# A key-value product with its high and low parts side by side, and a softmax-free attention's denominators in other places

## The chip, the cores and the metric

The kernel runs on one core of a Trainium2 chip. A core has a matrix engine (TensorE, PE in the profile, with its weight loads shown apart as PEld), a vector engine (VectorE, DVE), an activation engine (ScalarE, ACT), a general engine (GpSimd, POOL), and a sync engine (SyncE, SP) that issues the transfers here. Each engine works through its own queue in order; semaphores make one queue wait for another. The metric is device time in microseconds (us) of one execution, as the median of several runs.

## What is computed

One transformer block with adaptive layer norm, on a sequence of 2048 tokens with 512 channels, in fp32. Its first half is linear attention with 32 heads of 16 channels:

```python
pq, pk = phi(q), phi(k)                 # phi(t) = (t + 1 if t > 0 else exp(t)) + 1e-6
kv  = einsum("bhsd,bhse->bhde", pk, v)  # one 16 x 16 matrix per head
z   = einsum("bhsd->bhd", pk)
num = einsum("bhqd,bhde->bhqe", pq, kv)
den = einsum("bhqd,bhd->bhq", pq, z) + 1e-6
x   = x + ga * ((num / den) @ wo)
```

The second half is a gated feed-forward layer, `x + gb * (((h @ w_gate) * (h @ w_up)) @ w_down)`, with h the normalised and modulated x again. The vectors sa, ca, ga, sb, cb, gb come from `silu(c) @ w_mod`.

## The kernel before

**Precision.** A matrix product of fp32 values is made of three products in a rounded 32-bit format (fp32r). Each operand is split into a high part, which ScalarE writes by a copy into fp32r, and a low part, which VectorE writes as the difference (`split`, lines 193 to 195). `product` (lines 203 to 209) then adds, for each block of the contraction, high by high (line 207), high by low (208) and low by high (209) in one PSUM bank.

**Tiles.** The sequence is 16 tiles of 128 tokens, in four chunks of four. Work on tile i of the queries is called q tile i here. Tiles in SBUF come from one pool of 94 buffers of 128 x 512 fp32; PSUM is four accumulator banks (`acc`) and four working banks (`bank`). A working bank is handed out again when its last reader is done, so a new product can wait for a VectorE instruction that reads an old one.

**Order.** Nothing is scheduled by a planner in this part: the program is written in the order in which each engine gets its instructions, and an engine's queue is the sequence of its instructions in the text. A step late on one queue holds all that stands behind it there.

**The stretch that matters** begins after the last key tile. The key side has by then accumulated, in four banks `tacc[k]`, the normalised input against phi(k), which with the value weights gives kv without ever forming v. The steps, with their lines:

- `den_z` (671 to 673) reduces the key sums zb to a constant part of the denominators.
- Lines 779 and 780 scale `tacc[k]` into four tiles f; line 784 splits each of these into a high and a low part, `tt[k]`, each 128 x 512.
- The key-value product, lines 788 to 791: for each group g of 128 output columns, and each block k, the three products of 128 columns each. That is 4 x 4 x 3 = 48 matrix products of 128 x 128 by 128 x 128, into the one bank `kvps`.
- `mod_row` (line 792, by 183 and 189) makes the row gb: two products of 512 columns and one ScalarE copy.
- `q_b` (line 376) ends phi for a q tile; `q_a` (lines 372 and 373) begins it; `proj` is the projection of a q tile, 12 products of 512 columns.
- Line 799 masks `kvps` to the heads' diagonal blocks; `split` then gives `kvp`.
- Denominators of chunk 0 (tiles j = 0 to 3): `den_p` (line 679) multiplies phi(q) by z, `den_r` (685) sums it per head, `den_a` is both; `den_b` (695, 696) adds the constant and takes the reciprocal; `den_c` (703) multiplies phi(q) by it. All of it is VectorE's.
- `w_out` (lines 762 to 772): for each group g the product of `kvp` with the output weights, then line 768 on VectorE times ga, then a split: the four tiles `wp`.
- `ready(i)` is `den_c(i)` and a transfer of the tile to DRAM (line 324); `move_in(i)` brings it back in four pieces (line 332) so that a blockwise transpose (`turn_v`, line 748) completes the transpose of q tile i. Tiles 0 and 1 are transposed on TensorE instead (`turn_a`, line 717). `turn_h` and `turn_l` (721 and 725) split a transposed tile.
- `y_a(i)` (line 841): 12 products of the transposed q tile's parts with `wp`, added to the residual. Its third product is the first to read the low part that `turn_l` writes. `y_a(0)` starts a run of `y_a(0)` to `y_a(3)`.
- The weights of the first feed-forward tiles are loaded on SP (line 113) behind `move_in(3)`; `scale_down` (line 891) is VectorE's first use of one.

In the program order after the key-value product stand: `mod_row`, `q_b(6)`, `q_b(7)`, denominators of tiles 0 and 1, projection 8, the mask, the denominators of tiles 2 and 3, then `q_a(8)`, projection 9, `q_b(8)`, `den_c(0)`, `ready(2)`, `move_in(2)`, `w_out(0, 1)`, `q_a(9)`, `w_out(2, 3)`, `den_c(1)`, `q_b(9)`, `ready(3)`, `move_in(3)`, projection 10, and a little later the transposes of tiles 0 and 1, projection 11 and `y_a(0)`.

Of the kernel before, what the change touches and what calls it, by code (L numbers as in the profile page):

```python
# [9 lines left out]
F32R = mybir.dt.float32r  # L10
AF = mybir.ActivationFunctionType
ALU = mybir.AluOpType
AX = mybir.AxisListType

P = 128
# [9 lines left out]
def tile_adaln_block(  # L25
# [12 lines left out]
    nc = tc.nc  # L38
    ctx.enter_context(tc.manual_schedule())
    _, S, D = x.shape  # L40
    F = w_gate.shape[1]
    KD = D // P
# [25 lines left out]
    def f32(ap):  # L68
        return ap.bitcast(F32)
# [3 lines left out]
    def T(p, tag, shape=(P, D), dt=F32, bufs=None):  # L73
        cnt[0] += 1
        return p.tile(list(shape), dt, tag="t" if p is tiles else tag, name=f"{tag}_{cnt[0]}", bufs=bufs)

    def B(tag, shape=(P, D), dt=F32):

        return T(tiles, tag, shape, dt)
# [4 lines left out]
    def bank():  # L84
        return T(ps_w, "bank")
# [8 lines left out]
    mask = consts.tile([P, P], F32, name="mask")  # L94
# [91 lines left out]
    def mod_row(v, pair):  # L186
        ps = row_sum(pair)
        t = consts.tile([P, D], F32, name=f"row{v}")
        nc.scalar.activation(t, ps, AF.Copy)
        return t  # L190


    def split(src, h, l, low=None):
        nc.scalar.activation(h, src, AF.Copy)  # L194
        (low or nc.vector).tensor_tensor(l, src, f32(h), op=ALU.subtract)  # L195

    def split_raw(raw, shape=(P, D), low=None):
        h = B("w", shape, F32R)
        l = B("w", shape, F32R)
        split(raw, h[:raw.shape[0]], l[:raw.shape[0]], low)  # L200
        return h, l

    def product(ps, pairs):

        n = len(pairs)
        for i, ((ah, al), (bh, bl)) in enumerate(pairs):
            nc.tensor.matmul(ps, ah, bh, start=i == 0, stop=False)  # L207
            nc.tensor.matmul(ps, ah, bl, start=False, stop=False)  # L208
            nc.tensor.matmul(ps, al, bh, start=False, stop=i == n - 1)  # L209

    def cut(pair, a, b):
        return pair[0][:, a:b], pair[1][:, a:b]
# [144 lines left out]
    wk, wq, wv = [], [], []  # L357
    kx, phk, phq, q_ps = {}, {}, {}, {}

    def proj(i, w, of=bank):  # L360

        ch, j = divmod(i, NJ)
        ps = of()
        rows = w is wq and i not in FLIPPED
        product(ps.rearrange("p (s q i) -> p s q i", q=NQ, i=BL) if rows else ps,
                [(cut(norm[ch].t[k], j * P, (j + 1) * P), tuple(by_row(x) for x in w[k]) if rows else w[k])
                 for k in range(KD)])
        return ps
# [6 lines left out]
    def phi_b(ps, t):  # L375
        nc.vector.scalar_tensor_tensor(t, ps, 0.0, t, op0=ALU.max, op1=ALU.add)
# [41 lines left out]
    def q_a(i, ps):  # L418
        phq[i] = B("h")
        q_ps[i] = ps  # L420
        phi_a(ps, phq[i])

    def q_b(i):
        phi_b(q_ps.pop(i), phq[i])
# [251 lines left out]
    def den_p(ch, *js, on=None):  # L676
        for j in js:
            pzs[ch, j] = B("f")
            (on or nc.gpsimd).tensor_tensor(pzs[ch, j], phq[ch * NJ + j], zq if ch * NJ + j in FLIPPED else zb, op=ALU.mult)

    def den_r(ch, *js):
        if ch not in dens:
            dens[ch] = T(small, "den", (P, NJ, NH))
        for j in js:
            nc.vector.reduce_sum(dens[ch][:, j], pzs.pop((ch, j)).rearrange("p (h i) -> p h i", i=DH), axis=AX.X)

    def den_a(ch, *js, on=None):

        for j in js:
            den_p(ch, j, on=on)  # L690
            den_r(ch, j)

    def den_b(ch, a=0, b=NJ):
        d = dens[ch][:, a:b]
        nc.vector.tensor_tensor(d, d, (den0q if ch * NJ + a in FLIPPED else den0).unsqueeze(1).to_broadcast([P, b - a, NH]), op=ALU.add)
        nc.vector.reciprocal(d, d)

    def den_c(*tiles):

        for i in tiles:  # L700
            ch, j = divmod(i, NJ)
            p3 = phq[i].rearrange("p (h i) -> p h i", i=DH)
            nc.vector.scalar_tensor_tensor(p3, p3, EPS_PHI, dens[ch][:, j].unsqueeze(2).to_broadcast([P, NH, DH]),
                                           op0=ALU.add, op1=ALU.mult)

    def q_tile(i):
        q_a(i, proj(i, wq))
# [27 lines left out]
    def move_out(*tiles):  # L735

        for i in tiles:
            moved[i] = lift_out(f"moved_{i}", phq.pop(i))

    def move_in(*tiles):  # L740

        for i in tiles:
            moved[i] = lift_in(moved[i])
# [12 lines left out]
    def ready(*tiles):  # L756
        den_c(*tiles)
        move_out(*tiles)
# [17 lines left out]
    fs, tt = [], []  # L776
    for k in range(KD):
        f = B("n")
        nc.scalar.activation(f, tacc[k], AF.Copy, scale=ca[:, k:k + 1])
        nc.vector.scalar_tensor_tensor(f, zb, sa[:, k:k + 1], f, op0=ALU.mult, op1=ALU.add)  # L780
        fs.append(f)
    for f in fs:
        tt.append((B("w", dt=F32R), B("w", dt=F32R)))
        split(f, *tt[-1])
    pairs[5] = split_raw(accs[5])
    q_a(6, ps)
    q_tile(7)
    kvps = bank()
    for g in range(KD):
        a, b = g * P, (g + 1) * P  # L790
        product(kvps[:, a:b], [(cut(wv[k], a, b), cut(tt[k], a, b)) for k in range(KD)])
    gb = mod_row(5, pairs[5])
    q_b(6)
    q_b(7)
    den_a(0, 0, 1, on=nc.vector)
    ps = proj(8, wq)
    kvp = (B("xh", dt=F32R), B("xl", dt=F32R))
    kvf = B("n")
    nc.vector.tensor_tensor(kvf.rearrange("p (g c) -> p g c", g=KD), kvps.rearrange("p (g c) -> p g c", g=KD),
                            mask.unsqueeze(1).to_broadcast([P, KD, P]), op=ALU.mult)  # L800
    den_p(0, 2, on=nc.vector)
    split(kvf, *kvp)
    den_r(0, 2)
    den_a(0, 3, on=nc.vector)
    den_b(0, 0, 2)
    den_b(0, 2, 4)
    q_a(8, ps)
    ps = proj(9, wq)
    q_b(8)
# [5 lines left out]
    w_out(2, 3)  # L815
    den_c(1)
    q_b(9)
    ready(3)
    move_in(3)
    q_tile(10)  # L820
# [96 lines left out]
    def gate_up(ch, f):  # L917

        n = fts[f][1]
        gps, ups = bank(), bank()  # L920
        for k in range(KD):
            hh, hl = norm2[ch].t[k]
            for w, ps in ((wf[f][0], gps), (wf[f][1], ups)):
                nc.tensor.matmul(ps[:n], w[0][:, k], hh, start=k == 0, stop=False)  # L924
                nc.tensor.matmul(ps[:n], w[0][:, k], hl, start=False, stop=False)  # L925
                nc.tensor.matmul(ps[:n], w[1][:, k], hh, start=False, stop=k == KD - 1)  # L926

        def rest(*between):
            g = B("phi")
            h = B("kh", dt=F32R)  # L930
            l = B("kl", dt=F32R)
            nc.scalar.activation(g[:n], gps[:n], AF.Copy)
            nc.vector.tensor_tensor(g[:n], ups[:n], g[:n], op=ALU.mult)
            for do in between:
                do()
            split(g[:n], h[:n], l[:n])
            hs[ch, f] = h, l
        return rest
# [385 lines left out]
    g = gate_up(0, f0)  # L1324
# [8 lines left out]
    g = gate_up(0, f1)  # L1333
# [16 lines left out]
    g = gate_up(0, f2)  # L1350
# [45 lines left out]
    g = gate_up(1, f0)  # L1396
# [5 lines left out]
    g = gate_up(1, f1)  # L1402
# [6 lines left out]
    g = gate_up(1, f2)  # L1409
# [125 lines left out]
```

## Time and profile before

| | |
|---|---|
| median of 3 runs | 548.7 us (548.34 to 549.4) |
| the profiled execution | 548.6 us |
| its span, first to last instruction | 546.9 us |
| TensorE busy | 540.3 us, 99% |
| VectorE busy | 381.9 us, 70% |
| ScalarE busy | 293.3 us, 54% |
| GpSimd busy | 204.4 us, 37% |
| granted TensorE clock | 1.00 |

The page lists busy time by engine, the span in 40 slices, the chain of work that ended last, and groups of instructions. The timeline lists instructions in order of time: start in us, duration in us, engine, line, operation, what it writes and reads, count, and in brackets how long the engine had been idle before it and who released it. Matrix products are pipelined, so their durations overlap: what counts is the distance from one start to the next. The same holds to a smaller degree on VectorE and ScalarE, whose next instruction begins a little before the last one is shown as ended.

### The profile page before, as it was taken

How to read it: one execution, taken by the hardware profiler on the slowest of the kernel's cores; microseconds unless marked ns; L12 is line 12 of the kernel's file. 1: busy time of each engine (PE TensorE's matmuls, PEld its weight loads, DVE VectorE, ACT ScalarE, POOL GpSimd, SP SyncE). 2: the span in 40 equal slices, each digit the busy share in tenths (PEclk: the TensorE clock that was granted, in tenths of full speed). 3: DMA queues.
4: the chain of work that ended last, by engine and by line, in shares of the span. 5: the costliest groups of instructions: out<-in, count | busy, mean ns of one | idle time of the engine just before them, and what ended most of it. 6: DMA issues, size and time to landing. Idle time of an engine off the chain costs nothing.

```text
span 546.9 us, 7392 instructions
## 1 busy us (share of the span) xinstructions
PE 540.3 (99%) x2432; PEld 442.6 (81%) x2432; DVE 381.9 (70%) x632; ACT 293.3 (54%) x541; POOL 204.4 (37%) x207
## 2 busy tenths in 40 slices
PE   7999999999999999999999999999999999999997
PEld 6788888888788878878888888877888888888886
DVE  6898779989989888779765677985444344434444
ACT  3696777646577774577675545444452444444210
POOL 2001010000012220075796566766666656446100
PEclk9999999999999999999999999999999999999999
DMA  7912426210165255846363161880443222100004
GB/s 277 374 40 86 146 93 216 97 58 2 39 196 166 67 203 160 292 136 160 111 167 104 42 190 38 284 260 36 120 124 108 58 59 58 59 19 1 0 1 155
DMA packets 68455, 65.65 MB, mean 120 GB/s; under 512 B 8448, under 2 KB 46592, under 8 KB 68416
## 3 DMA queue, kind: packets, MB, share of 16 engines
q1 hardware_dynamic: 68416, 65.17, 37.8%
q8 instruction: 19, 0.31, 0.2%
q14 instruction: 20, 0.16, 0.1%
HBM read 46.27 MB, written 18.87 MB: 119 GB/s over the span
## 4 chain that ended last, share of the span: by engine, by line
PE 96%; DMA 2%; DVE 1%; ACT 0%; issue 0%; SPq 0%
PE bank L1100 33%; PE acc L841 7%; PE acc L1181 6%; PE acc L1180 6%; PE acc L1182 6%; PE bank L207 4%; PE bank L209 4%; PE bank L208 4%; PE acc L416 3%; PE acc L414 3%; PE acc L415 3%; PE bank L924 2%; PE bank L926 2%; PE bank L925 2%; DMA raw<-in_w_mod_dram 1%; PE acc L951 1%
## 5 line engine op out<-in xcount | busy, mean ns | idle before, releaser
L1100 PE MATMUL bank<-h,w 128*128 128x512 f32 (+1 forms) x798 | 184.7, 390 | 0.0
L1100 PEld LDWEIGHTS bank<-h,w 128*128 128x128 f32 (+1 forms) x798 | 148.4, 186 | 33.3 <-ACT bank L1105 0.6
L1105 ACT ACTIVATE bank<-bank 128x512 f32<-128x512 f32 (+1 forms) x38 | 22.2, 583 | 139.5 <-PE bank L1100 139.3
L911 DVE TENSOR_TENSOR x<-acc,x 128x512 f32<-128x512 f32 (+1 forms) x73 | 48.8, 682 | 49.6 <-PE acc L1182 47.7
L1086 POOL TENSOR_TENSOR w<-raw,w 128x256 fp32r<-128x256 f32 (+3 forms) x38 | 40.8, 1074 | 91.2 <-ACT w L1079 91.2
L195 POOL TENSOR_TENSOR w<-raw,w 128x512 fp32r<-128x512 f32 (+1 forms) x26 | 36.5, 1405 | 67.1 <-ACT w L194 62.2
L1180 PE MATMUL acc<-w,kh 128*128 128x512 f32 (+2 forms) x154 | 59.6, 387 | 0.0
L1181 PE MATMUL acc<-w,kh 128*128 128x512 f32 (+2 forms) x154 | 59.6, 387 | 0.0
L1182 PE MATMUL acc<-w,kl 128*128 128x512 f32 (+2 forms) x154 | 59.5, 386 | 0.0
L263 POOL TENSOR_TENSOR rstd<-ve,half 128x2 f32<-128x2 f32 (+3 forms) x13 | 12.2, 939 | 109.5 <-DVE ve L262 44.8
L1086 POOL TENSOR_TENSOR w<-t,w 128x512 fp32r<-128x512 f32 (+1 forms) x38 | 49.2, 1313 | 0.0
L195 DVE TENSOR_TENSOR kl<-u,kh 128x512 fp32r<-128x512 f32 (+1 forms) x38 | 26.4, 735 | 30.9 <-ACT kh L194 30.9
L207 PE MATMUL bank<-w,h 128*128 128x512 f32 x104 | 40.8, 392 | 0.0
L209 PE MATMUL bank<-w,h 128*128 128x512 f32 x104 | 40.7, 391 | 0.0
L208 PE MATMUL bank<-w,h 128*128 128x512 f32 x104 | 40.5, 390 | 0.0
L841 PE MATMUL acc<-w,xh 128*128 128x512 f32 x120 | 37.1, 390 | 0.0
L1159 DVE TENSOR_TENSOR u<-bank,u 128x512 f32<-128x512 f32 (+1 forms) x19 | 13.1, 691 | 31.1 <-PE bank L1100 23.8
L1180 PEld LDWEIGHTS acc<-w,kh 128*128 128x128 f32 (+1 forms) x154 | 28.9, 188 | 6.0
L1181 PEld LDWEIGHTS acc<-w,kh 128*128 128x128 f32 (+1 forms) x154 | 28.9, 188 | 5.9
L1182 PEld LDWEIGHTS acc<-w,kl 128*128 128x128 f32 (+1 forms) x154 | 28.9, 188 | 5.9
L1068 POOL TENSOR_TENSOR t<-raw,t 128x256 f32<-128x256 f32 (+1 forms) x34 | 25.8, 759 | 1.3
L841 PEld LDWEIGHTS acc<-w,xh 128*128 128x128 f32 x120 | 22.5, 188 | 4.6
(216 smaller groups left out, 1108.9 us busy)
## 6 DMA issues: line engine op xcount, KB each, us to landing
raw<-in_w_mod_dram SPq DMA_DIRECT2D x24, 256.0 KB, 3.6
raw<-in_B_w_down_dram SPq DMA_DIRECT2D x20, 256.0 KB, 2.8
raw<-in_B_w_gate_dram SPq DMA_DIRECT2D x36, 128.0 KB, 3.5
raw<-in_B_w_up_dram SPq DMA_DIRECT2D x36, 128.0 KB, 3.5
x<-in_A_x_dram SPq DMA_DIRECT2D x16, 256.0 KB, 5.4
out_dram<-x SPq DMA_DIRECT2D x15, 256.0 KB, 2.7
moved<-h SPq DMA_DIRECT2D x14, 256.0 KB, 2.1
u<-moved SPq DMA_DIRECT2D x56, 64.0 KB, 2.0
```

What stands on the lines that cost most here:

```text
L195: (low or nc.vector).tensor_tensor(l, src, f32(h), op=ALU.subtract)
L207: nc.tensor.matmul(ps, ah, bh, start=i == 0, stop=False)
L208: nc.tensor.matmul(ps, ah, bl, start=False, stop=False)
L209: nc.tensor.matmul(ps, al, bh, start=False, stop=i == n - 1)
L841: nc.tensor.matmul(yps[i], x, y, start=False, stop=k == KD - 1 and x is al, skip_group_check=True)
L911: nc.vector.tensor_tensor(xt[:, a:b], dn[j][:, a:b], xt[:, a:b], op=ALU.add)
L1068: sub = lambda out, x, y: (on or nc.gpsimd).tensor_tensor(out, x, y, op=ALU.subtract)
L1086: sub = lambda out, x, y: (on or nc.gpsimd).tensor_tensor(out, x, f32(y), op=ALU.subtract)
L1100: mm = lambda x, y, **kw: nc.tensor.matmul(ps, x[:, k], y, skip_group_check=True, **kw)
L1180: nc.tensor.matmul(ps, hh[:, a:b], dh[:n, c:d], start=i == 0, stop=False)
L1181: nc.tensor.matmul(ps, hh[:, a:b], dl[:n, c:d], start=False, stop=False)
L1182: nc.tensor.matmul(ps, hl[:, a:b], dh[:n, c:d], start=False, stop=i == len(hs) - 1)
```

## The change

The four tiles f are split in another layout. Instead of a high tile and a low tile of 512 columns, each f gives two tiles; each of these holds, for two groups of 128 columns, the high part and the low part next to each other. So a slice of 256 columns is high and low of one group. The splits become eight ScalarE copies and eight VectorE subtractions of 256 columns in place of four and four of 512.

The product then takes, for each group g and block k, one matrix product of 256 columns (high of the weights against high and low) and one of 128 columns (low of the weights against high). Its result lies in two banks in place of one: for each group, 128 columns with high by high plus low by high, and 128 columns with high by low. ScalarE copies the second kind out of PSUM (once per bank), VectorE adds it to the first (once per bank), and the mask is a separate VectorE operation on 512 columns in SBUF.

The denominators of chunk 0 move as well. Tile 1's pair of operations (`den_a`) now stands behind the mask; `den_b` of tiles 0 and 1 behind `kvp`'s split; then tile 2's `den_a` and its own `den_b`. Tile 3's `den_a` and `den_b` stand further back, behind `q_b(9)` and ahead of `ready(3)`.

```diff
+    NG = KD // 2
     for f in fs:
-        tt.append((B("w", dt=F32R), B("w", dt=F32R)))
-        split(f, *tt[-1])
+        both = [B("w", dt=F32R).rearrange("p (g t c) -> p g t c", g=NG, t=2) for _ in range(KD // NG)]
+        for n, u in enumerate(both):
+            part = f[:, n * NG * P:(n + 1) * NG * P].rearrange("p (g c) -> p g c", g=NG)
+            nc.scalar.activation(u[:, :, 0], part, AF.Copy)
+            nc.vector.tensor_tensor(u[:, :, 1], part, f32(u[:, :, 0]), op=ALU.subtract)
+        tt.append(both)
     pairs[5] = split_raw(accs[5])
     q_a(6, ps)
     q_tile(7)
-    kvps = bank()
+    kvps = [bank().rearrange("p (g t c) -> p g t c", g=NG, t=2) for _ in range(KD // NG)]
     for g in range(KD):
-        a, b = g * P, (g + 1) * P
-        product(kvps[:, a:b], [(cut(wv[k], a, b), cut(tt[k], a, b)) for k in range(KD)])
+        n, i = divmod(g, NG)
+        for k in range(KD):
+            (vh, vl), t = cut(wv[k], g * P, (g + 1) * P), tt[k][n][:, i]
+            nc.tensor.matmul(kvps[n][:, i], vh, t, start=k == 0, stop=False, skip_group_check=True)
+            nc.tensor.matmul(kvps[n][:, i, 0], vl, t[:, 0], start=False, stop=k == KD - 1, skip_group_check=True)
     gb = mod_row(5, pairs[5])
     q_b(6)
     q_b(7)
-    den_a(0, 0, 1, on=nc.vector)
+    den_a(0, 0, on=nc.vector)
     ps = proj(8, wq)
     kvp = (B("xh", dt=F32R), B("xl", dt=F32R))
     kvf = B("n")
-    nc.vector.tensor_tensor(kvf.rearrange("p (g c) -> p g c", g=KD), kvps.rearrange("p (g c) -> p g c", g=KD),
-                            mask.unsqueeze(1).to_broadcast([P, KD, P]), op=ALU.mult)
-    den_p(0, 2, on=nc.vector)
+    kv3 = kvf.rearrange("p (g c) -> p g c", g=KD)
+    low = B("f").rearrange("p (g c) -> p g c", g=KD)
+    for n, x in enumerate(kvps):
+        a, b = n * NG, (n + 1) * NG
+        nc.scalar.activation(low[:, a:b], x[:, :, 1], AF.Copy)
+        nc.vector.tensor_tensor(kv3[:, a:b], x[:, :, 0], low[:, a:b], op=ALU.add)
+    nc.vector.tensor_tensor(kv3, kv3, mask.unsqueeze(1).to_broadcast([P, KD, P]), op=ALU.mult)
+    den_a(0, 1, on=nc.vector)
     split(kvf, *kvp)
-    den_r(0, 2)
-    den_a(0, 3, on=nc.vector)
     den_b(0, 0, 2)
-    den_b(0, 2, 4)
+    den_a(0, 2, on=nc.vector)
+    den_b(0, 2, 3)
     q_a(8, ps)
...
     den_c(1)
     q_b(9)
+    den_a(0, 3, on=nc.vector)
+    den_b(0, 3, 4)
     ready(3)
     move_in(3)
```

## The prediction

> **What bounds the kernel now.** I read the page's busy times first, then the waits of TensorE's weight loads, then the timelines of TensorE and VectorE around the change.
>
> ```profile
> span 546.9 us, 7392 instructions
> PE 540.3 (99%) x2432; PEld 442.6 (81%) x2432; DVE 381.9 (70%) x632; ACT 293.3 (54%) x541; POOL 204.4 (37%) x207
> ```
>
> TensorE is busy for all but 6.6 us, so a microsecond of its work or of its waiting is about a microsecond of the whole, unless another engine makes it wait anyway. That happens once in the stretch of the change:
>
> ```profile
> 144.99 0.19 PEld L207 LDWEIGHTS bank<-w,xh 128*128 128x128 f32 x1 [0.50 <-DVE n L768]
> ```
>
> This is the fourth output-weight product; its PSUM bank is free only when VectorE has read the first one (line 768). VectorE's queue up to there is almost without a gap:
>
> ```profile
> 136.93 0.69 DVE L799 TENSOR_TENSOR n<-bank,mask 128x512 f32<-128x512 f32 x1 [0.69 <-PE bank L209]
> 137.54 0.68 DVE L679 TENSOR_TENSOR f<-h,z 128x512 f32<-128x512 f32 x1
> 138.59 0.69 DVE L195 TENSOR_TENSOR xl<-n,xh 128x512 fp32r<-128x512 f32 x1 [0.37 <-ACT xh L194]
> 139.20 0.68 DVE L685 TENSOR_REDUCE den<-f 128x32 f32<-128x512 f32 x1
> 139.80 0.68 DVE L679 TENSOR_TENSOR f<-h,z 128x512 f32<-128x512 f32 x1
> 140.52 0.69 DVE L685 TENSOR_REDUCE den<-f 128x32 f32<-128x512 f32 x1
> 141.12 0.22 DVE L695 TENSOR_TENSOR den<-den,den 128x64 f32<-128x64 f32 x1
> 141.37 0.55 DVE L696 RECIPROCAL den<-den 128x64 f32<-128x64 f32 x1
> 141.84 0.16 DVE L695 TENSOR_TENSOR den<-den,den0q 128x64 f32<-128x64 f32 x1
> 142.04 0.55 DVE L696 RECIPROCAL den<-den 128x64 f32<-128x64 f32 x1
> 142.50 0.63 DVE L376 SCALAR_TENSOR_TENSOR h<-bank,h 128x512 f32<-128x512 f32 x1
> 143.05 1.28 DVE L703 SCALAR_TENSOR_TENSOR h<-h,den 128x512 f32<-128x512 f32 x2
> 144.25 1.28 DVE L768 TENSOR_TENSOR n<-bank,row 128x512 f32<-128x512 f32 x2
> ```
>
> The reader is to see that from the key-value product's end to line 768 VectorE, not TensorE, sets the time. It stays so up to the low part of q tile 0 (line 725), which `y_a(0)` reads in its third product:
>
> ```profile
> 150.03 0.68 DVE L376 SCALAR_TENSOR_TENSOR h<-bank,h 128x512 f32<-128x512 f32 x1
> 150.63 0.68 DVE L703 SCALAR_TENSOR_TENSOR h<-h,den 128x512 f32<-128x512 f32 x1
> 151.23 0.68 DVE L725 TENSOR_TENSOR xl<-bank,xh 128x512 fp32r<-128x512 f32 x1
> ```
> ```profile
> 152.64 0.40 PE L841 MATMUL acc<-w,xl 128*128 128x512 f32 x1
> ```
>
> The low part ends at 151.91 and is read at 152.64: 0.73 us to spare before, and no more.
>
> **The product on TensorE.**
>
> ```profile
> 131.42 0.22 PE L207 MATMUL bank<-w,w 128*128 128x128 f32 x1
> ```
> ```profile
> 136.62 0.28 PE L209 MATMUL bank<-w,w 128*128 128x128 f32 x1
> 136.73 0.45 PE L183 MATMUL bank<-w,ones_r 128*128 128x512 f32 x1
> ```
>
> 48 products of 128 columns take 136.73 - 131.42 = 5.31 us, 0.111 each. The kernel's last output tile has products of 256 columns with a weight load each, the first and the last of twelve being
>
> ```profile
> 541.74 0.28 PE L1180 MATMUL acc<-w,kh 128*128 128x256 f32 x1
> ```
> ```profile
> 543.05 0.28 PE L1182 MATMUL acc<-w,kl 128*128 128x256 f32 x1
> ```
>
> so (543.05 - 541.74) / 11 = 0.119 each. The new product is 16 x 0.119 + 16 x 0.111 = 3.68 us: 1.63 us less, and the row gb starts at 135.10 in place of 136.73.
>
> A rule of the Trainium skill speaks against this gain: TensorE: Matmul & The Clock Gate, section Back-to-back issue gap, gives for a product by itself N / 2.4 + 2.5 ns; as an estimate from that page 55.8 ns for 128 columns and 109 for 256, thus 2.68 us before and 2.64 after, no gain at all. This trace disagrees: 5.31 us, not 2.68. Its section on LDWEIGHTS (columns / 1.2, 107 ns for 128) lies near the 0.111 instead.
>
> **The splits ahead of it.** Eight VectorE subtractions of 256 columns replace four of 512, and eight ScalarE copies four.
>
> ```profile
> 128.88 2.49 DVE L195 TENSOR_TENSOR w<-n,w 128x512 fp32r<-128x512 f32 x4
> ```
> ```profile
> 233.10 0.42 DVE L1068 TENSOR_TENSOR t<-raw,t 128x256 f32<-128x256 f32 x1
> 233.44 0.42 DVE L1068 TENSOR_TENSOR t<-raw,raw 128x256 f32<-128x256 f32 x1
> ```
>
> A VectorE operation on 256 columns comes 0.34 after the last one. Eight from 128.88 end near 131.7; the fourth block's first half is the seventh and ends near 131.3, while the product wants it at 131.42 + 3 x 0.23 = 132.1. Cost nothing, hidden behind projection 7; without that cover it would be 8 x 0.34 - 4 x 0.60 = 0.3 us. That the pieces are strided (128 columns of every 256) no row shows: between 0.34 and the 0.60 of a whole 512-column operation, I take 0.34.
>
> **From the product to the mask.** The old mask read PSUM the moment the product ended. The new chain has a step on ScalarE, and there the copies (line 811) stand in the queue behind the row gb's copy, which waits for the product and for two more products.
>
> ```profile
> 137.44 0.60 ACT L189 ACTIVATE row<-bank 128x512 f32<-128x512 f32 x1 [4.56 <-PE bank L183]
> 137.94 0.62 ACT L194 ACTIVATE xh<-n 128x512 fp32r<-128x512 f32 x1
> ```
> ```profile
> 244.85 0.41 ACT L1079 ACTIVATE w<-raw 128x256 fp32r<-128x256 f32 x1
> ```
>
> The row's copy starts 0.71 after its first product (137.44 - 136.73), so at 135.81; the next ScalarE instruction 0.50 later, at 136.31. A copy of 256 columns out of PSUM is not in the trace: bounds 0.41 (from SBUF) and the 0.60 of 512 columns; I take 0.41, the nearer shape. VectorE's first addition (line 812) starts at about 136.77. So of the 1.63 us that TensorE gains, VectorE gets 136.93 - 136.77 = 0.16; tile 1's denominators no longer fill that gap.
>
> **VectorE's queue from there,** start to start, durations from the rows above (an operation that reads the one before starts 0.04 after its end): addition 0.34, addition 0.46, mask 0.61, tile 1's line 679 0.72 and 685 0.60, `kvp`'s low part 0.60, lines 695 and 696 on 64 columns 0.25 and 0.47, tile 2's 679 and 685 0.72 and 0.72, 695 0.20, 696 on 32 columns, `q_b(8)` 0.55, two of line 703 1.20. The reciprocal on 32 columns is new:
>
> ```profile
> L696 DVE RECIPROCAL den<-den x6: 553/553/953, 141.4 to 223.6; 128x64 f32<-128x64 f32 x4, 128x128 f32<-128x128 f32 x2
> ```
>
> 64 columns take 0.553 and 128 take 0.953, so by the line through them 32 take 0.353 (bounds 0.2 and 0.55), next start 0.26 later. Sum: 7.70 us. Line 768 starts at 136.77 + 7.70 = 144.47, before at 144.25: 0.2 us later. TensorE, although it arrives 1.6 us earlier, waits for `q_b(8)` and for line 768 and starts its fourth product about 0.2 later than before. The whole gain is gone there.
>
> **Tile 3's denominators.** They now stand between `q_b(9)` and `den_c(3)`, ahead of q tile 0's low part: 0.72 + 0.72 + 0.20 + 0.39 (line 703 reads the reciprocal) = 2.03 us. Line 725 starts at 151.23 + 0.22 + 2.03 = 153.48 and ends at 154.17. TensorE reaches `y_a(0)` 0.2 later than before, and its third product starts at about 154.20 in place of 152.64. At 144.99 a product that starts together with its weight load is 0.11 longer:
>
> ```profile
> 144.99 0.50 PE L207 MATMUL bank<-w,xh 128*128 128x512 f32 x1
> ```
>
> (0.50 against 0.39 to 0.40). So TensorE goes on 1.56 + 0.11 = 1.67 us late.
>
> **What is queued behind.** q tile 3's move to DRAM on SP waits for `den_c(3)`, and the first feed-forward loads stand behind it:
>
> ```profile
> 151.34 0.34 SPq L324 DMA_DIRECT2D moved<-h  x1
> ```
> ```profile
> 156.34 0.50 SPq L113 DMA_DIRECT2D raw<-in_B_w_down_dram  x1
> ```
> ```profile
> 161.58 0.68 DVE L891 TENSOR_TENSOR raw<-raw,row 128x512 f32<-128x512 f32 x1
> ```
>
> All of it goes 2.25 us later, five transfers and nine loads. The tile has until `y_a(3)`, itself 1.67 later. The first down weights have 161.58 - 156.34 = 5.24 us from issue to use; later issue by 2.25 against a use that VectorE reaches some 1 to 1.7 later leaves 4.1 to 4.7. The same kind of loads took
>
> ```profile
> raw<-in_B_w_down_dram SPq DMA_DIRECT2D x2, 256.0 KB, 5.1
> ```
>
> in that window, so VectorE may wait about a microsecond at line 891. TensorE itself is then 1.67 late; I take nothing for it, 0 to 0.6 us as bounds. GpSimd gets nothing new. After the stretch TensorE has no idle time that could take up 1.67 us, so it reaches the end.
>
> **Sum.** 0 from the product (its 1.63 lost at line 768), +0.22 for VectorE's longer queue, +2.03 for tile 3's denominators, -0.73 that was to spare less what waiting adds (0.03 + 0.11): 1.67, or +1.7 us on the profiled 548.6, whose span was 546.9. The median is 548.7, 0.1 above it: 550.4 us.
>
> **Rivals.**
> - *TensorE's gain survives* (faster): q tile 0's low part would be there in time. It decides at line 725's end: by 151.0 (152.64 less the 1.63 of the product). The kernel then keeps 1.63 and the 0.2 to 0.3 us of the wait at 144.99: 546.8 us. Against it: VectorE must lose 3 us of work that the rows count. For it: only that VectorE's starts are from other shapes.
> - *No measurable change.* A measurement tells 0.2% (1.1 us) from nothing. If VectorE's chain is 0.6 us shorter than counted (the addition starts at 136.5, a reciprocal of 0.2, no 0.04 steps), line 725 ends near 153.5: about 549.7.
> - *The product ends late* (slower): strided pieces at 0.60 let the last split end near 133.8, or products of 256 columns gain nothing; then the whole chain from line 189 starts 1.0 to 1.6 us later: 551.4 to 552.0. Against it: the rows of 0.119 at the kernel's end.
> - *The late loads reach TensorE*: up to 0.6 more, 551.0.
>
> **How the numbers follow.** Forecast (549.8 to 551.0) 0.66; no measurable change 0.15; gain survives 0.07; product late 0.07; loads 0.05. Slower by over 0.2%: 0.66 + 0.07 + 0.05 = 0.78; within 0.15; faster 0.07. The range leaves out the faster case and about half of the late product: 548.8 to 551.6.
>
> **What would show it.** Right: 32 products in about 3.7 us; line 189 at about 135.8, line 812 at 136.8; VectorE idle for nearly 2 us ahead of it; weight loads waiting for `q_b(8)` and line 768 for about 2 us together; `y_a(0)` waiting for line 725 for about 1.5 us. Wrong: line 725 ending before 153, no wait in `y_a(0)`, or a product of 5 us. What would make it wrong most easily is VectorE's pace on shapes the trace lacks.

## The result and the profile after

The changed kernel takes 550.27 us (median of 7 runs, 550.12 to 550.93), the kernel before in the same comparison 548.54 us (median of 7, 548.06 to 549.4). The ratio is 1.0028, with a 95% interval of 1.0016 to 1.0041: 1.7 us slower. The profiled execution of the changed kernel took 550.13 us and has a span of 548.4 us. Its count of time begins 0.26 us later in the program than that of before: what stands ahead of the change carries times that are 0.26 smaller, and the key-value product starts at 131.16 in place of 131.42. So 0.26 is added where its times are set beside those of before.

The page of the changed kernel begins:

```profile
span 548.4 us, 7373 instructions
PE 540.1 (98%) x2416; PEld 441.5 (81%) x2416; DVE 383.3 (70%) x640; ACT 294.3 (54%) x547; POOL 204.8 (37%) x207
```

TensorE has 16 products fewer, yet its idle time goes from 6.6 to 8.3 us. TensorE's timeline at both ends of the new product, and ScalarE's behind it:

```profile
131.16 0.28 PE L798 MATMUL bank<-w,w 128*128 128x256 f32 x1
...
134.80 0.45 PE L183 MATMUL bank<-w,ones_r 128*128 128x512 f32 x1
```
```profile
135.53 0.60 ACT L189 ACTIVATE row<-bank 128x512 f32<-128x512 f32 x1 [2.91 <-PE bank L183]
136.02 0.66 ACT L811 ACTIVATE f<-bank 128x256 f32<-128x256 f32 x2
```

The product takes 134.80 - 131.16 = 3.64 us instead of 5.31. VectorE's timeline behind it, and the weight loads that waited:

```profile
136.43 0.76 DVE L812 TENSOR_TENSOR n<-bank,f 128x256 f32<-128x256 f32 x2 [1.77 <-ACT f L811]
...
142.08 0.35 DVE L696 RECIPROCAL den<-den 128x32 f32<-128x32 f32 x1
142.35 0.63 DVE L376 SCALAR_TENSOR_TENSOR h<-bank,h 128x512 f32<-128x512 f32 x1
142.90 1.28 DVE L703 SCALAR_TENSOR_TENSOR h<-h,den 128x512 f32<-128x512 f32 x2
144.10 1.28 DVE L768 TENSOR_TENSOR n<-bank,row 128x512 f32<-128x512 f32 x2
...
150.49 0.68 DVE L679 TENSOR_TENSOR f<-h,z 128x512 f32<-128x512 f32 x1
151.20 0.69 DVE L685 TENSOR_REDUCE den<-f 128x32 f32<-128x512 f32 x1
...
153.15 0.68 DVE L725 TENSOR_TENSOR xl<-bank,xh 128x512 fp32r<-128x512 f32 x1
```
```profile
143.03 0.19 PEld L207 LDWEIGHTS bank<-w,xh 128*128 128x128 f32 x1 [1.12 <-DVE h L376]
144.83 0.19 PEld L207 LDWEIGHTS bank<-w,xh 128*128 128x128 f32 x1 [1.27 <-DVE n L768]
153.88 0.19 PEld L855 LDWEIGHTS acc<-w,xl 128*128 128x128 f32 x1 [1.63 <-DVE xl L725]
```

The reader is to see VectorE idle for 1.77 us right behind the shorter product, and then TensorE waiting for VectorE three times: 1.12 and 1.27 us where there had been 0.50 in all, and 1.63 us in `y_a(0)` where there had been nothing. The first two take back the gain; the third is the loss.

### The profile page after: what moved, and what is told of

The parts are those of the page before. It is cut to its first block, busy times and chain, and to the rows that moved or that the text cites. A ratio compares the mean times of both kernels' runs of the same rounds, so it can differ in the third digit from the quotient of the medians.

```text
span 548.4 us, 7373 instructions
## 1 busy us (share of the span) xinstructions
PE 540.1 (98%) x2416; PEld 441.5 (81%) x2416; DVE 383.3 (70%) x640; ACT 294.3 (54%) x547; POOL 204.8 (37%) x207
## 4 chain that ended last, share of the span: by engine, by line
PE 96%; DVE 3%; ACT 0%; issue 0%
PE bank L1114 33%; PE acc L855 7%; PE acc L1195 6%; PE acc L1194 6%; PE acc L1196 6%; PE bank L209 4%; PE bank L207 4%; PE bank L208 4%; PE acc L416 3%; PE acc L414 3%; PE acc L415 3%; PE bank L938 2%; PE bank L940 2%; PE bank L939 2%; PE acc L146 2%; PE acc L965 1%
```

## The experiments

Two distances are used below, both from TensorE's timeline: A, from the start of the first key-value product to the start of `y_a(0)`'s third product, the stretch that the change edits; and B, from there to the start of the kernel's last matrix product. They do not depend on where an execution's count of time begins. Both are read from one profiled execution of each kernel, while the ratio is that of the medians of several. Executions of one kernel can lie 2 us apart (the kernel before took 548.14 to 550.43 us in one of the comparisons), so a difference in B of a microsecond or less counts only where a row shows the wait behind it. In four of the profiled executions (narrow products, loads behind, both with GpSimd) the granted clock was 0.66 from 15 to 20 us, ahead of everything that the change touches; that is in their times, but in neither A nor B.

| kernel | A, us | B, us | ratio of times to the kernel before |
|---|---|---|---|
| before | 152.64 - 131.42 = 21.22 | 543.05 - 152.64 = 390.41 | 1 |
| changed | 153.88 - 131.16 = 22.72 | 390.69 | 1.0028 [1.0016, 1.0041] |
| product alone | 21.52 | 390.46 | 0.9999 [0.999, 1.0008] |
| denominators alone | 22.17 | 391.47 | 1.0034 [1.0022, 1.0046] |
| row later | 21.39 | 390.53 | 1.0 [0.9991, 1.0009] |
| narrow products | 24.37 | 391.53 | 1.0065 [1.0047, 1.0083] |
| tile 3 behind the low part | 22.91 | 392.98 | 1.0099 [1.0084, 1.0113] |
| the same, loads behind it | 21.35 | 391.83 | 1.0033 [1.002, 1.0046] |
| GpSimd products, new order | 21.14 | 391.47 | 1.0001 [0.9987, 1.0015] |
| GpSimd products, old order | 21.33 | 390.73 | 1.0004 [0.9992, 1.0016] |
| reordered queue, early loads | 19.25 | 396.95 | 1.0078 [1.0065, 1.0091] |
| reordered queue, loads late | 19.25 | 393.00 | 0.9979 [0.9971, 0.9988] |
| reordered, early loads, old product | 20.91 | 397.84 | 1.0125 [1.0105, 1.0146] |
| reordered, loads late, old product | 20.91 | 392.96 | 1.0043 [1.0029, 1.0057] |

The theory: VectorE's queue sets the time from the product to q tile 0's low part, so the shorter product brings nothing and tile 3's denominators ahead of the low part cost what they last. The rivals: the product itself is slower in some way, or the loss is elsewhere.

### One part of the change at a time

Product alone, against the changed kernel:

```diff
-    den_a(0, 0, on=nc.vector)
+    den_a(0, 0, 1, on=nc.vector)
...
-    den_a(0, 1, on=nc.vector)
+    den_p(0, 2, on=nc.vector)
     split(kvf, *kvp)
-    den_b(0, 0, 2)
-    den_a(0, 2, on=nc.vector)
-    den_b(0, 2, 3)
+    den_r(0, 2)
+    den_a(0, 3, on=nc.vector)
+    den_b(0, 0, 2)
+    den_b(0, 2, 4)
...
-    den_a(0, 3, on=nc.vector)
-    den_b(0, 3, 4)
     ready(3)
```

> The new product, splits and evacuation, with all denominators in their old places (tile 1 ahead of the mask, tiles 2 and 3 right behind it). Theory (VectorE's queue sets the time, and tile 3's late denominators are what costs): the first addition still waits for ScalarE until about 136.4, tile 1's denominators fill the gap ahead of it, the two additions make VectorE's queue up to line 768 about 0.3 us longer than before, and y_a(0) waits for nothing. 0.3 us over the kernel before, ratio 1.0005 (1.000 to 1.001). Rival (the product with its extra ScalarE step is what costs): all of the 1.7 us, ratio 1.003.

Denominators alone is the reverse: these lines of the change on the kernel before, with its old product.

> The old product and mask, with the denominators in their new places. Theory: line 768 comes 0.4 us earlier than before, but tile 3's 2.0 us of denominators stand ahead of q tile 0's low part, which ends at about 153.6 in the times of the profile before; y_a(0) waits about 1.4 us for it. 1.0 us over the kernel before, ratio 1.0019 (1.001 to 1.003). Rival (the product costs): no change or a little faster, ratio 0.999 to 1.000.

The product alone measured 0.9999: neither a gain nor a loss. Its weight loads wait for the same two VectorE instructions:

```profile
PEld bank L207 <- DVE h L376: 1.3, 1, 1.3
PEld bank L207 <- DVE n L768: 1.3, 1, 1.3
```

(waits of the weight loads in us in total, times, longest). 2.6 us of waiting stand where 0.5 stood, and none in `y_a(0)`. The denominators alone measured 1.0034, all of the loss. In the stretch they cost 22.17 - 21.22 = 0.95 us, near the 1.0 that had been expected for the whole; B is 1.06 us longer as well, which was not expected. VectorE's timeline, GpSimd's, and a weight load in that kernel:

```profile
163.43 1.18 DVE L892 TENSOR_TENSOR raw<-raw,row 128x512 f32<-128x512 f32 x1 [1.18 <-DMA raw<-in_B_w_down_dram]
...
180.11 1.82 DVE L316 TENSOR_TENSOR h<-f,h 128x512 fp32r<-128x512 f32 x1
```
```profile
180.10 2.99 POOL L195 TENSOR_TENSOR w<-raw,w 128x512 fp32r<-128x512 f32 x2 [4.23 <-ACT w L194]
```
```profile
181.99 0.19 PEld L926 LDWEIGHTS bank<-h,w 128*128 128x128 f32 x1 [0.81 <-DVE h L316]
```

VectorE waits for the down weights, and 18 us later TensorE for VectorE. This is the rival of the late loads, but with a step between: the last line 316 takes 1.82 us, where the others take 0.69, beside two subtractions that GpSimd has begun 0.01 us before it. At 0.69 it would have ended at 180.80, before TensorE asked for it (181.99 - 0.81 = 181.18). In the changed kernel line 316 is done (179.28 to 179.97) before GpSimd begins (180.12), and TensorE does not wait there. The same is seen wherever this wait appears below: line 316 has 1.83 us in the narrow products and 1.69 in both kernels with loads late. That VectorE comes to line 316 late because of the down weights is argued from the order of its queue. In the changed kernel these loads are issued as far behind `y_a(0)`'s third product (158.21 - 153.88 = 4.33 us, here 158.16 - 153.85 = 4.31) and VectorE waits for them only 0.19 us; the two larger ones took 4.7 us there and 5.9 here (median of the two in the window), so the size of this loss hangs on how long the transfers take in an execution.

### Is the product's end the start of the chain?

Narrow products: each product of 256 columns is two of 128, in the changed kernel.

```diff
-            nc.tensor.matmul(kvps[n][:, i], vh, t, start=k == 0, stop=False, skip_group_check=True)
+            nc.tensor.matmul(kvps[n][:, i, 0], vh, t[:, 0], start=k == 0, stop=False, skip_group_check=True)
+            nc.tensor.matmul(kvps[n][:, i, 1], vh, t[:, 1], start=k == 0, stop=False, skip_group_check=True)
```

In this kernel the two halves of a group begin their sums separately in one bank, and the sums in it are not those of the reference; the instructions and their order are those described.

> The changed kernel in its new layout, but each product of 256 columns is two of 128 columns again (high and low of one group, 48 products in all). Theory (the time that TensorE saves in the product is lost later, but the row gb, ScalarE's copies and VectorE's additions are anchored on the product's end, so in the changed order they would all start later without it): the product takes 48 x 0.111 = 5.3 us in place of 3.64, the first addition starts 1.6 us later, and so does q tile 0's low part: 1.6 us over the changed kernel, a ratio to the kernel before of about 1.006. Rival (the length of the product does not matter at all, since VectorE sets the time): the same as the changed kernel, 1.003.

Measured 1.0065, and A grows by 24.37 - 22.72 = 1.65 us (B by another 0.84, with a wait of 0.8 us for line 316 as in the denominators alone). So in the changed order the product's length does matter, one for one: the row's copy, ScalarE's copies and VectorE's additions all wait for its end. Without the 1.63 us that the new product saves, the new order would have lost that too.

Row later: `mod_row` moved between `q_a(8)` and projection 9, so that ScalarE's copies of the product do not queue behind the row's copy.

```diff
-    gb = mod_row(5, pairs[5])
     q_b(6)
...
     q_a(8, ps)
+    gb = mod_row(5, pairs[5])
     ps = proj(9, wq)
```

> The changed kernel, with the row gb (two products and its ScalarE copy) between projections 8 and 9 rather than right behind the key-value product, so that the copies out of PSUM do not stand behind it on ScalarE. Theory: the second addition starts at about 135.4 rather than 136.8, the whole VectorE queue behind it 1.3 us earlier, q tile 0's low part too; y_a(0) still waits about 1.3 us. 1.3 us under the changed kernel, ratio to the kernel before 1.0007 (1.000 to 1.0015). Rival (VectorE's queue is set further back, by q_b(8) or the output-weight products): no gain, ratio 1.003.

Measured 1.000: the whole loss is undone by moving one step of two products and a copy. The first addition starts 3.43 us behind the product's start (134.81 - 131.38) in place of 5.27. The second, which waits for ScalarE's second copy, starts at 135.64, and line 768 and line 725 follow 1.3 us earlier than in the changed kernel. The waits of the weight loads:

```profile
PEld acc L855 <- DVE xl L725: 1.6, 1, 1.6
PEld bank L207 <- DVE n L768: 0.9, 1, 0.9
```

A falls from 22.72 to 21.39. The wait in `y_a(0)` stays at 1.6, because TensorE comes there earlier by as much.

### Taking the wait in y_a(0) away

Tile 3 behind the low part: its four steps behind `turn_l(0)`, in the changed kernel.

```diff
-    den_a(0, 3, on=nc.vector)
-    den_b(0, 3, 4)
-    ready(3)
-    move_in(3)
     q_tile(10)
...
     turn_l(0)
+    den_a(0, 3, on=nc.vector)
+    den_b(0, 3, 4)
+    ready(3)
+    move_in(3)
     y_seed(0)
```

> The changed kernel, with tile 3's denominators, its scaling, its move to DRAM and back all behind q tile 0's low part. Theory: the 1.6 us wait of y_a(0) goes (1.35 us of TensorE time plus 0.11), but tile 3's move leaves 0.6 us later while TensorE comes 1.4 us earlier, so y_a(3) now waits 0.3 to 0.9 us for q tile 3. 0.5 to 1.0 us under the changed kernel, ratio to the kernel before 1.001 to 1.0025. Rival (the wait at y_a(0) only shows a loss that comes from the product): no gain, ratio 1.003.

Measured 1.0099: 4 us over the changed kernel, where 0.5 to 1.0 under it had been expected. The wait in `y_a(0)` was gone, but two things came in its place. First, the nine feed-forward loads stood ahead of the move on SP now, and tile 3 came late to `y_a(3)`:

```profile
163.86 0.30 PEld L851 LDWEIGHTS acc<-w,xh 128*128 128x128 f32 x2 [2.18 <-ACT acc L842]
```

Second, the granted clock fell (columns: stretch, its length, then each engine's busy time, and at the end the granted clock, the DMA share and GB/s):

```profile
141.00:145.00 4.00, 2.46 (x11) 1.41 (x9) 3.90 (x9) 0.06 (x1) 0.00 (x0) 1.00 0.00 0
145.00:149.00 4.00, 4.00 (x11) 3.15 (x12) 3.80 (x7) 3.52 (x6) 0.00 (x0) 0.57 0.36 119
149.00:153.00 4.00, 4.00 (x21) 3.32 (x20) 2.64 (x5) 2.20 (x4) 0.00 (x0) 1.00 0.92 253
```

Twenty-one products in four microseconds at full clock, eleven at 0.57. This follows two waits, 1.12 us for `q_b(8)` and 1.27 us for line 768, that the changed kernel has as well, and there the clock stayed at 1.00. All four executions of this kernel have a mean clock of 0.997 or less, six of the seven of the changed one 0.999 or more. Why the clock falls in the one and not in the other is not shown.

The same with the loads behind tile 3's move (`for f in lone: load_ffn(f)` moved there from its old place) keeps SP's order (`lone` are the first three feed-forward tiles, with three loads each).

> As the run in which tile 3's denominators stood behind q tile 0's low part, but the feed-forward loads are issued behind tile 3's move, as in the changed kernel, so that the move does not queue behind nine loads. Theory: the wait of 1.6 us in y_a(0) goes, and y_a(3) waits for its own transposed tile: the move goes out at about 153.9, the four pieces at 156.0, the transpose starts at about 159.5, its high part is there at 160.8 and y_a(3) comes to it at about 160.1, so 0.3 to 0.9 us of waiting there; 0.6 to 1.3 us under the changed kernel, a ratio to the kernel before of 1.0005 to 1.002. Rival (the half clock of the earlier run comes from the two waits at 142 and 144 in this order of the program, whatever the transfers do): the clock falls again and the time is over the changed kernel, 1.004 to 1.006.

Measured 1.0033, the same as the changed kernel within the intervals. In the profiled execution the clock stayed at 1.00 in the stretch, so the rival of the expectation falls for it. A falls by 22.72 - 21.35 = 1.37 us, but B grows by 1.14: `y_a(3)` waits. The weight load and ScalarE's timeline:

```profile
162.09 0.30 PEld L851 LDWEIGHTS acc<-w,xh 128*128 128x128 f32 x2 [1.19 <-ACT acc L842]
```
```profile
160.92 0.63 ACT L721 ACTIVATE xh<-f 128x512 fp32r<-128x512 f32 x1 [1.28 <-DVE f L748]
161.45 0.58 ACT L842 ACTIVATE acc<-x 128x512 f32<-128x512 f32 x1
```

The expectation had 0.3 to 0.9 there. The move was not late: it goes out 154.68 - 131.99 = 22.69 us behind the product's start, and the expected 153.9 is 22.74 behind that of the changed kernel (131.16). But the expectation let `y_a(3)` start with its high part (line 721); it waits for line 842, ScalarE's copy of the residual into its accumulator, which stands behind line 721 in ScalarE's queue. The wait was only moved from tile 0 to tile 3.

### Giving VectorE's work to GpSimd

GpSimd is idle from 125.5 to 161.7 in the row-later kernel. There the products of line 679 for tiles 2 and 3 are given to it:

```diff
     pairs[5] = split_raw(accs[5])
+    den_p(0, 2, 3)
     q_a(6, ps)
...
-    den_a(0, 2, on=nc.vector)
+    den_r(0, 2)
...
-    den_a(0, 3, on=nc.vector)
+    den_r(0, 3)
```

> The changed kernel with the row gb behind q_a(8) (as in the earlier run, 1.000) and with two of VectorE's operations taken off its queue: the products of phi(q) and z for tiles 2 and 3 (line 679) run on GpSimd, which is idle there from 125 on. Theory (from the product to q tile 0's low part VectorE's queue alone sets the time): line 768 starts 0.7 us earlier than with the row moved alone, line 725 1.4 us earlier; the wait of 0.9 us for line 768 shrinks to about 0.2 and the end comes 1.4 us earlier: about 547.6 us, a ratio to the kernel before of 0.9975 (0.996 to 0.999). Rival (something else waits there, or GpSimd's work beside VectorE's slows VectorE by what it saves): no gain, 1.000 or more.

The second kernel does the same with the denominators in their old order (tile 2's sum ahead of `kvp`'s split, tile 3's behind it, one `den_b(0, 2, 4)`).

> The new product with the row gb behind q_a(8), the denominators in the old places (tile 3's ahead of line 768, one pair of lines 695 and 696 for tiles 2 and 3), and the products of tiles 2 and 3 on GpSimd. Theory: line 768 starts about 0.6 us earlier than with the row moved alone in the changed order, TensorE waits 0.3 us or less there, and q tile 0's low part is done before TensorE asks for it, so nothing is lost in y_a(0): the end comes about 2.1 us earlier than with the row moved alone, 546.9 us, a ratio to the kernel before of 0.996 (0.995 to 0.998); most of the 1.6 us that the product saves then shows. Rival (the product's gain cannot be had, since another wait takes its place): 0.999 to 1.001.

Measured 1.0001 and 1.0004: no gain. The timelines of VectorE and of GpSimd in the first of them:

```profile
126.72 1.00 DVE L672 TENSOR_SCALAR den<-den 128x32 f32<-128x32 f32 x1
127.75 1.22 DVE L673 COPY den0q<-den 128x32 f32<-128x32 f32 x1
128.89 2.73 DVE L780 SCALAR_TENSOR_TENSOR n<-zb,col,n 128x512 f32<-128x512 f32 x4
```
```profile
126.38 2.55 POOL L679 TENSOR_TENSOR f<-h,z 128x512 f32<-128x512 f32 x2
```

Two operations of 32 columns, 0.18 us each in the kernel before, take 1.00 and 1.22 us, and line 780 starts as GpSimd's work ends (126.38 + 2.55 = 128.93). Everything behind is 1.9 us later on VectorE, and the product now waits for its splits three times, 1.0 us in all, where it had not waited. VectorE lost at its head what it was to save behind. The rival of that expectation holds.

### VectorE's queue in TensorE's order

The last four kernels give nothing away; they write VectorE's queue in the order in which TensorE needs its results. The order behind the mask, with the row later (`w_out` here is the product, line 768 and ScalarE's high part; `w_low` are the low parts that `w_out` had made before; with the loads late, `load_ffn(lone[0])` is not there and all of `lone` is loaded behind `move_in(3)`; the lines that were taken away are left out here):

```diff
+    den_p(0, 1, on=nc.vector)
     split(kvf, *kvp)
+    den_r(0, 1)
+    den_a(0, 2, on=nc.vector)
     q_a(8, ps)
+    gb = mod_row(5, pairs[5])
     ps = proj(9, wq)
     q_b(8)
+    den_a(0, 3, on=nc.vector)
+    q_a(9, ps)
+    for g in range(KD):
+        w_out(g)
+    den_b(0, 0, 2)
     den_c(0)
+    den_b(0, 2, 4)
     ready(2)
     move_in(2)
+    q_b(9)
     den_c(1)
+    load_ffn(lone[0])
+    w_low(0, 1)
     q_tile(10)
...
     turn_l(0)
+    ready(3)
+    move_in(3)
+    for f in lone[1:]:
+        load_ffn(f)
+    w_low(2, 3)
     y_seed(0)
```

> The new product, with VectorE's queue written in the order in which TensorE needs its results, and nothing given to another engine: the row gb behind q_a(8); q_b(8) ahead of tile 3's denominators; the four output-weight products and line 768 together and ahead of all den_b and den_c; the low parts of the output weights for the third and fourth block and den_c(3) with its move behind q tile 0's low part; the first feed-forward tile's three loads ahead of tile 3's move. Theory (the product's 1.6 us are there, but VectorE's order hides them): line 768 starts at about 142.0 in the time of the run with the product alone (144.18 there), no wait of TensorE for line 768 or q_b(8), q tile 0's low part starts at about 149.4 (151.17 there), y_a(0) reaches its third product at about 150.3 in place of 152.59: 2.3 us less, 546.3 us, a ratio to the kernel before of 0.996 (0.9945 to 0.998). Rival (the work only moves: the tile 3 that is late, or the loads, make TensorE wait for as much): 0.999 or more.

> As the reordered queue, but all nine feed-forward loads stand behind tile 3's move. Theory (the first feed-forward weights are on the edge already before; denominators alone lost 0.8 us to them): they are issued some 0.6 us earlier than before while TensorE and VectorE come to them 2.3 us earlier, so VectorE waits about 1.5 us at its scaling of the down weights and TensorE loses 0.5 to 1.0 us: a ratio to the kernel before of 0.9975 (0.996 to 0.999). Rival (VectorE's wait there is covered by its slack): as the reordered queue with the early loads, 0.996.

> The same reordered queue and early loads with the old product of 48 times 128 columns, its mask straight from PSUM. Theory (the product's own gain is 1.63 us and shows only where VectorE does not set the time): TensorE has no wait any more in this stretch, so the 0.5 us of the wait before goes, and its product stays 1.63 us longer: about 548.1 us, a ratio to the kernel before of 0.999 (0.998 to 1.000), 1.6 us over the reordered queue with the new product. Rival (the order alone makes the gain and the product none): the same time as with the new product.

> The reordered queue with all nine loads behind tile 3's move (0.9979 with the new product) and the old product of 48 times 128 columns in place of the new one. Theory (with VectorE out of the way the product's 1.6 us are TensorE's): from the product's first instruction to y_a(0)'s third product 20.9 us as in the run with early loads (19.25 with the new product, 21.22 before), so 0.3 us under before at that point; the loads are then less late and VectorE's wait of 0.75 us for the down weights goes, so not all of the difference of 1.65 us to the new product reaches the end: 548.6 to 549.2 us, a ratio to the kernel before of 0.9985 to 1.000. Rival (the order alone makes the gain): 0.998 as with the new product.

In the stretch itself the theory holds to 0.4 us. VectorE's timeline with early loads (line 775 is line 768 of the other kernels), and the weight load of `y_a(0)`'s third product:

```profile
141.64 2.73 DVE L775 TENSOR_TENSOR n<-bank,row 128x512 f32<-128x512 f32 x4
...
149.59 0.68 DVE L725 TENSOR_TENSOR xl<-bank,xh 128x512 fp32r<-128x512 f32 x1
```
```profile
150.33 0.19 PEld L867 LDWEIGHTS acc<-w,xl 128*128 128x128 f32 x1 [0.28 <-DVE xl L725]
```

Line 768 was expected at 142.0, the low part at 149.4, the third product at 150.3. A is 19.25 us with the new product and 20.91 with the old, in both pairs. So the product's gain is there, 1.66 us, as soon as TensorE does not wait for `q_b(8)` and line 768; the wait of 0.28 us for line 725 is there with either product. With the reordered queue and the old product A gains only 0.31 on the kernel before. The rival (the order alone makes the gain) falls in the stretch.

What comes behind the stretch went otherwise. With the early loads, 1.0078: three loads of 256 KB are under way when tile 3's move is issued.

```profile
151.29 0.40 SPq L113 DMA_DIRECT2D raw<-in_B_w_gate_dram  x1
...
152.85 0.42 SPq L324 DMA_DIRECT2D moved<-h  x1
157.35 1.75 SPq L332 DMA_DIRECT2D u<-moved  x4
```
```profile
162.70 0.72 PE L867 MATMUL acc<-w,xh 128*128 128x512 f32 x2 [3.99 <-ACT acc L858]
```
```profile
164.00:168.00 4.00, 4.00 (x12) 3.14 (x12) 3.97 (x5) 3.11 (x9) 2.98 (x2) 0.61 0.31 94
```

The pieces can be fetched 4.5 us after the move's issue, with free queues 2.1 (151.50 to 153.63 in the loads-late kernel). TensorE stands for 4.0 us in `y_a(3)` (its weight loads for 4.4), and then runs at a clock of 0.61. The old product with early loads has the same wait (4.6 us) and an even longer stretch of low clock.

With the loads late, 0.9979 [0.9971, 0.9988]: 547.92 us (median of 12, 547.3 to 549.31) against 549.22. This is a version that beats both kernels. VectorE's wait for the down weights is 0.75 us, where about 1.5 was expected. The waits of the weight loads between 150 and 190 us:

```profile
PEld acc L859 <- ACT acc L850: 0.9, 2, 0.7
PEld bank L943 <- DVE h L316: 0.8, 1, 0.8
PEld acc L859 <- DVE xl L725: 0.6, 2, 0.3
PEld bank L293 <- ACT n L272: 0.6, 1, 0.6
PEld acc L859 <- DVE w L777: 0.2, 1, 0.2
PEld bank L942 <- ACT f L305: 0.2, 1, 0.2
```

The gain in the stretch is 21.22 - 19.25 = 1.97 us; in the profiled execution B is 2.59 us longer, so this execution (549.11 us) kept nothing, while the median of the twelve is 1.3 us under the kernel before. The other executions must have lost less behind the stretch; which of these waits were shorter in them, no trace shows, and that stays open. The 0.8 us for line 316 are again an operation that begins just behind GpSimd's (178.56 and 178.40).

The old product with the loads late: 1.0043, where 0.9985 to 1.000 was expected. The step of this expectation that failed is the one about the loads: they were to be less late, but they are issued behind tile 3's move, which stands behind the product like all the rest, and everything is later together. B is 392.96 against 393.00 with the new product. So the whole 1.62 us of the product reach the end in the two profiled executions (A + B 413.87 against 412.25). The medians lie further apart, 550.98 - 547.92 = 3.06 us: the profiled execution of the new product (549.11) lies 1.19 over its median, that of the old one (550.63) 0.35 under. The ratios add 0.4 us to it, since the kernel before had 548.79 in the one comparison and 549.22 in the other. Why the executions differ, no trace shows.

## Why the prediction was right

The forecast was 550.4 us, 1.7 over before; 550.27 us, also 1.7 over, was measured. Step by step (0.26 added to the times after):

| step | forecast | measured |
|---|---|---|
| 32 products | 3.68 us | 3.64 us |
| row's copy, line 189 | 135.81 | 135.79 |
| ScalarE's copy, line 811 | 136.31 | 136.28 |
| first addition, line 812 | 136.77 | 136.69 |
| reciprocal of 32 columns | 0.353 us | 0.35 us |
| line 768 | 144.47 | 144.36 |
| waits for `q_b(8)` and line 768 | about 2 us | 1.12 + 1.27 us |
| line 725 | 153.48 | 153.41 |
| third product of `y_a(0)` | 154.20, 1.56 late | 154.14, 1.50 late |
| the kernel's last product | 1.67 late | 544.57 + 0.26 - 543.05 = 1.78 late |

Every start in the stretch lies within 0.11 us of its forecast, so the time is not right by luck. Only in the last 0.1 us there is some: the stretch came out 0.06 us short, and what stands behind it took 0.28 longer where 0.11 was forecast.

- *The product's gain is lost at line 768.* Shown: with the product alone the time is that of before and the waits are 2.6 us; with VectorE's queue reordered the gain of 1.66 us appears.
- *The chain hangs on ScalarE's queue behind the row.* Shown: with the row moved, the loss is gone.
- *Tile 3's denominators cost 2.03 us, of which 0.73 are to spare.* Shown by the denominators alone in the stretch (0.95 us late, 1.0 expected there).
- *Cost of the splits: nothing.* Right: the eight subtractions end before the product needs them, with no wait at its first products. When GpSimd's work held VectorE up by 1.9 us this cover was gone, and the product waited 1.0 us.
- *VectorE may wait about a microsecond for the down weights; nothing for TensorE.* Mis-sized: 0.19 us was measured. The loads went out 2.13 us later (158.21 + 0.26 against 156.34), where 2.25 was worked out, but landed in 4.3 us (162.47 - 158.21) and not in 5.1. (The time left to them comes to 4.0 to 4.7 us by the prediction's own numbers, not 4.1 to 4.7.) In the denominators alone the same loads took longer, and TensorE lost about a microsecond behind the stretch, 0.8 of it at line 316: the rival of the late loads, which had 0 to 0.6, was sized too low there, and GpSimd's part in it was not seen.
- The rivals: the gain did not survive in this order, and the product did not end late. Of the last, the narrow products show that 1.6 us of product would indeed have cost 1.65 more.

The rule that had spoken against the gain (the Trainium skill, TensorE: Matmul & The Clock Gate, section Back-to-back issue gap) is N / 2.4 + 2.5 ns for a product by itself, and the same section says that it counts too little for small N in a stream of products with a weight load each. By the formula alone the two forms would be equal. It does not hold for this stream: the new product took 3.64 us against 5.31, and with 128 columns only the stretch became 1.65 us longer.

## What to carry to other kernels

Before shortening an engine's work, follow the queue of the engine that it will wait for next: a gain of 1.6 us on TensorE came out as nothing, and showed only when VectorE's queue was written in the order in which TensorE needs its results. A step moved "behind" the critical work on one engine is ahead of something else there, and takes its transfers past other transfers on their queue: count what stands behind it on both. The cheapest repair may be a step that has nothing to do with the change; here it was a row's copy that stood ahead of the product's copies in ScalarE's queue.

## What the hardware showed that was not expected

- While GpSimd ran two operations on 128 x 512 (2.55 us from 126.38), two VectorE operations of 32 columns took 1.00 and 1.22 us in place of 0.18 each; the second ended at 128.97, GpSimd's work at 128.93. A VectorE operation of 0.69 us that began 0.01 us behind one of GpSimd's took 1.82. The Trainium skill, SBUF — State Buffer, section "SBUF: two separate sides", says that the two engines share a pair of ports under an exclusive lock that is held for a whole instruction (of VectorE's instructions, those with two SBUF inputs or in a mode with two ports); the trace agrees.
- The granted clock fell to 0.57 over 4 us behind two waits of 1.12 and 1.27 us in one kernel, and stayed at 1.00 behind the same two waits in the changed one; behind a wait of 4.4 us it fell to 0.61. The Trainium skill, TensorE: Matmul & The Clock Gate, Part 1, has a window of 3413 ns that runs freely, and lets the clock fall after an idle window. The wait of 4.4 us fits this; two waits of 2.39 us together, with products between them, make no idle window, and why the clock fell behind them stays open.
- A 256 KB move to DRAM was ready to be fetched after 4.5 us when three loads of 256 KB had been issued in the 1.6 us before it, and after 2.1 us without them.
